# Tiles that begin at a multiple of 256 bytes: filling up the first pool on each side of SBUF

## The chip, the cores and the metric

One NeuronCore of a Trainium2 chip runs the whole kernel. The metric is the device time of one execution in microseconds (us). A changed kernel is compared with the kernel before by the ratio of their times.

## The reference

Three layers run one after the other, all in float32.

```python
# attention with a sigmoid: batch 4, 12 heads, 448 positions, head size 64
scores = scale * q @ k.T - log(448)
attn = 1 / (1 + exp(-scores))
x = (attn @ v) laid out as [1792 tokens, 768]
# max of three products, then an output product (768 x 768 each)
h = max(x @ w1, x @ w2, x @ w3)
x = h @ w_out
# a layer with a leaky slope per column (768 x 2048 and 2048 x 768)
h = x @ w_in
g = max(h, 0) + alpha * min(h, 0)
out = g @ w_out2
```

The weights arrive as float64, which the kernel reads as pairs of 32-bit words and turns into float32 itself.

## The kernel before, in words

All matmuls of the two feed-forward layers are products of float32 numbers that were split into a high and a low part of type fp32r. Each product is three matmuls: high by low, low by high, high by high. A matmul has a **stationary** operand, 128 columns that a weight load (LDWEIGHTS) brings in, and a **moving** operand whose columns are then streamed past it. There is one weight load for each matmul.

The stages are named after their PSUM tiles:

- attention, up to about 146 us: `sc` (scores, L461, moving operand `qh` or `ql`, two matmuls side by side on 64 rows each) and `pav` (L482, plain float32, moving operand `a`);
- `b`, 146 to 399 us (`product`, L641, through `group`, L599 to L604): 1,134 matmuls with 448 moving columns. Names `b_0X`, `b_1X` and so on carry the half g = 0 or g = 1 of the batch as their number. The moving operand is `x_...h` or `x_...l`, the stationary one `f_...h` or `f_...l`;
- `c`, 376 to 467 us (`c_group`, L696): 432 matmuls with 448 moving columns, moving operand `h_...`;
- `d` and `e`, 467 to 933 us, eight rounds: `d` (`d_group`, L833) streams `yh` or `yl`, 512 columns in 948 matmuls and 256 columns in 120; `e` (`e_tile`, L856) streams `g_...`, 512 columns in 864; `e_short` (L884) streams 384 columns of weights in 192.

Weights come in through `wr` (L97 to L117, DMAs on SP's queue); ACT and DVE turn them into `wt` and split them (L177 to L217). `hd` and `hr` (L636, L689) park one intermediate in DRAM and fetch it back.

**Where the tiles lie.** SBUF is filled from two sides, and every pool places its tiles in multiples of 32 bytes of a partition's row. On the left stand the DMA scratch (`SCRATCH`, 4,096 bytes), four constants of 32 bytes each, and then the pool `const` (L63, from byte 4,224): `bias_s` takes 32 bytes, `alpha_sb` and `nalpha` 64 each. So everything behind it begins at 4,384 = 17 x 256 + 32: `wpool` (all weights, raw and split), then `slots_b` and, in its place later, `gpool`. All their tiles are multiples of 256 bytes long, so each begins 32 bytes behind a multiple of 256. On the right the first pool ends at byte 229,344 = 895 x 256 + 224 and is filled downward: `slots_a`, then `apool` and later `slots_c`; `ypool` takes their place for the last layer. These tiles begin 224 bytes behind a multiple of 256, and those of `apool` below the 16-byte tile `gate` (`kh`, `kl` and `zeros`) 192 bytes behind one.

So the moving operand of a matmul begins 32 bytes behind a multiple of 256 in `e`, in `c`, and in `b` for g = 0; 224 bytes behind one in `d`, in the `sc` and `pav` of attention, and in part of `b` for g = 1 (L288: r = 1 lies in `slots_a`, r = 2 mostly in `slots_c`). The stationary operand of `b`, `c` and `d`, and of `e` outside `e_short`, lies in `wpool`, at 32. Slices within a tile begin at multiples of 256 bytes from its start.

The order of the instructions is fixed by the program: a list of products (L737 to L747), and a queue of small operations that are issued between them by credits (`advance`, L135).

Of the kernel before, what the change touches and what calls it, by code (L numbers as in the profile page):

```python
# [9 lines left out]
F32 = mybir.dt.float32  # L10
# [6 lines left out]
P = 128  # L17
# [4 lines left out]
def kernel(  # L22
# [26 lines left out]
    KF2 = DF2 // P  # L49
# [11 lines left out]
    neg_log_s = -math.log(S)  # L61

    const = ctx.enter_context(tc.tile_pool(name="const", bufs=1))  # L63
    wpool = ctx.enter_context(tc.tile_pool(name="wpool", bufs=1))
    pools = {}
    room = {"a": 28, "b": 48, "c": 24, "y": 4}
# [4 lines left out]
    def wslot(nm, dt=F32):  # L71
        return wpool.tile([P, HF], dt, tag="ws", name=nm, bufs=23)

    bias_s = const.tile([P, 1], F32, name="bias_s")
    alpha_sb = const.tile([P, KF2], F32, name="alpha_sb")
    nalpha = const.tile([P, KF2], F32, name="nalpha")

# [242 lines left out]
    def attention(apool, ps_s, ps_v):  # L322
# [187 lines left out]
        nc.vector.memset(bias_s, neg_log_s)  # L510
        zeros = apool.tile([P, 512], BF16, tag="zeros", name="zeros")
        nc.vector.memset(zeros, 0.0)
        gate = apool.tile([P, 4], F32, tag="gate", name="gate")
        ident = apool.tile([P, P], F32, tag="ident", name="ident")
        nc.gpsimd.memset(ident, 0.0)
        nc.gpsimd.affine_select(
# [449 lines left out]
    with tc.manual_schedule():  # L966
        dpool = ctx.enter_context(tc.tile_pool(name="hstore", bufs=1, space=bass.MemoryType.DRAM))
        right = ExitStack()
        pools["a"] = right.enter_context(tc.tile_pool(name="slots_a", bufs=1, side="right"))
        with tc.tile_pool(name="slots_b", bufs=1) as pools["b"]:  # L970
            with (
                tc.tile_pool(name="apool", bufs=1, side="right") as apool,
                tc.tile_pool(name="ps_s", bufs=3, space=bass.MemoryType.PSUM) as ps_s,
                tc.tile_pool(name="ps_v", bufs=2, space=bass.MemoryType.PSUM) as ps_v,
            ):
                attention(apool, ps_s, ps_v)
            ps_m = ctx.enter_context(
                tc.tile_pool(name="ps_m", bufs=8, space=bass.MemoryType.PSUM, reuse_waits="tile")
            )
            pools["c"] = right.enter_context(  # L980
                tc.tile_pool(name="slots_c", bufs=1, side="right", reuse_waits="tile")
            )

            def swap():
                right.close()
                pools["y"] = ctx.enter_context(
                    tc.tile_pool(name="ypool", bufs=1, side="right", reuse_waits="tile")
                )

            z0 = ff1(ps_m, dpool, swap)  # L990
        with tc.tile_pool(name="gpool", bufs=1, reuse_waits="tile") as gpool:
            ff2(gpool, ps_m, z0)
# [39 lines left out]
```

## Time and profile before

| | before |
|---|---|
| median of 3 runs | 942.4 us (940.82 to 943.27) |
| the profiled execution's own time | 942.17 us |
| its span, from the first to the last instruction | 940.4 us |
| PE (matmul) busy | 927.1 us, 99% |
| DVE, ACT, POOL busy | 613.8, 446.8, 71.7 us |
| granted TensorE clock | 0.999 |

A busy PE is one with matmuls in flight. Their ends are modelled and they overlap, so the pace of a stage is read from the starts of its matmuls: time of a stretch divided by the matmuls in it. [...]

### The profile page before, as it was taken

What the parts mean: (1) busy time and instruction counts of PE and PEld (TensorE: products, weight loads), DVE (VectorE), ACT (ScalarE), POOL (GpSimd) and SP (SyncE); (2) the same over time, 40 slices, a digit from 0 to 9 for tenths busy, and PEclk for the clock granted to TensorE, in tenths of its full rate; (3) what the DMA queues carried; (4) which work ended last, traced back from release to release, by engine and by line L of the source; (5) the groups of instructions that cost most, each with busy time, mean ns of one, the idle gap of its engine ahead of it and who ended that gap; (6) DMA issues with size and microseconds to landing.
All of it is one profiled execution on the core that took longest, in us unless ns stands there. A gap on an engine that the chain in (4) does not pass through costs nothing.

```text
span 940.4 us, 12606 instructions
## 1 busy us (share of the span) xinstructions
PE 927.1 (99%) x4712; PEld 758.5 (81%) x4712; DVE 613.8 (65%) x1187; ACT 446.8 (48%) x878; POOL 71.7 (8%) x115
## 2 busy tenths in 40 slices
PE   8999989999999999999999999999999999999997
PEld 5555547999999999899988888888888888888886
DVE  5888885776566568743464466686666866568675
ACT  5878886534433446433366550634506345163410
POOL 4433310001001001100000000000000000000001
PEclk9999999999999999999999999999999999999999
DMA  8999670423114224321221211212112121122027
GB/s 147 141 163 143 114 122 17 118 82 115 49 46 136 68 68 146 112 65 37 68 68 51 67 35 51 67 51 68 34 51 68 51 69 32 51 68 60 25 58 178
DMA packets 148573, 74.24 MB, mean 79 GB/s; under 512 B 94128, under 2 KB 144656, under 8 KB 148512
## 3 DMA queue, kind: packets, MB, share of 16 engines
q1 hardware_dynamic: 140704, 57.60, 27.1%
q0 software_dynamic: 5664, 14.98, 5.7%
q10 hardware_dynamic: 2144, 0.85, 0.4%
q8 instruction: 37, 0.61, 0.3%
q14 instruction: 24, 0.20, 0.1%
HBM read 64.23 MB, written 9.18 MB: 78 GB/s over the span
## 4 chain that ended last, share of the span: by engine, by line
PE 94%; DVE 2%; DMA 1%; ACT 1%; SPq 1%; issue 0%; DVEq 0%; ACTq 0%
PE d L601 25%; PE e L601 21%; PE c L601 9%; PE b_0X L601 7%; PE b_1X L601 7%; PE sc L461 5%; PE pav L482 5%; PE b_0W L601 4%; PE e_short L903 4%; PE b_1W L601 3%; PE b_0V L601 2%; PE b_1V L601 2%; DMA kr<-in_k_dram 1%; ACT a L472 1%; SPq L402 1%
## 5 line engine op out<-in xcount | busy, mean ns | idle before, releaser
L817 DVE SCALAR_TENSOR_TENSOR r<-n,nalpha,r 128x512 f32<-128x512 f32 (+1 forms) x64 | 43.1, 683 | 106.1 <-ACT n L814 106.1
L876 DVE TENSOR_TENSOR acc<-e,acc 128x512 f32<-128x512 f32 x126 | 86.7, 688 | 24.1 <-PE e L601 21.9
L813 ACT ACTIVATE r<-d 128x512 f32<-128x512 f32 (+1 forms) x50 | 29.6, 591 | 152.5 <-PE d L601 152.5
L472 ACT ACTIVATE a<-sc,bias_s 128x896 f32<-128x896 f32 x84 | 82.1, 1015 | 15.1 <-PE sc L461 14.9
L482 PE MATMUL pav<-a,vt 128*64 128x448 f32 (+1 forms) x384 | 70.3, 551 | 0.0
L185 ACT ACTIVATE wt<-wr 128x384 f32<-128x384 f32 x112 | 61.9, 553 | 12.6 <-DMA wr<-in_moe_w_dram 6.3
L200 DVE CUSTOM_DVE_ANT_0 wt<-wr,wt 128x768 uint16<-128x768 uint16 x112 | 62.5, 558 | 3.9
L192 DVE SCALAR_TENSOR_TENSOR wr<-wr 128x384 uint32<-128x384 uint32 x112 | 62.0, 554 | 1.1
L188 ACT ACTIVATE wr<-wr 128x384 uint32<-128x384 uint32 x112 | 61.8, 552 | 0.0
L482 PEld LDWEIGHTS pav<-a,vt 128*64 128x64 f32 (+1 forms) x384 | 21.0, 135 | 38.6 <-issue 35.4
L191 DVE TENSOR_SCALAR wt<-wt 128x384 uint32<-128x384 uint32 x112 | 39.8, 356 | 14.2 <-ACT wt L185 14.2
L931 POOL DMA_DIRECT2D out_dram<-o x6 | 3.9, 660 | 531.3 <-DVE o L851 531.3
L461 PE MATMUL sc<-qh,kh 64*128 64x448 f32 x192 | 38.3, 395 | 4.6 <-DVE qh L435 2.4
L722 DVE TENSOR_TENSOR yl<-c,yh 128x448 fp32r<-128x448 f32 (+5 forms) x36 | 14.1, 421 | 41.5 <-ACT yh L718 29.8
L383 POOL DMA_DIRECT2D vt<-in_v_dram x46 | 35.3, 770 | 65.3 <-PE pav L482 65.3
L461 PEld LDWEIGHTS sc<-qh,kh 64*128 64x128 f32 x192 | 18.1, 184 | 23.2 <-issue 5.6
L718 ACT CAST yh<-c 128x448 fp32r<-128x448 f32 (+5 forms) x36 | 12.1, 375 | 50.1 <-PE c L601 50.1
L461 PE MATMUL sc<-ql,kh 64*128 64x448 f32 x192 | 35.7, 368 | 0.0
L461 PE MATMUL sc<-qh,kl 64*128 64x448 f32 x192 | 35.4, 365 | 0.0
L814 ACT ACTIVATE n<-d 128x512 f32<-128x512 f32 (+1 forms) x50 | 29.2, 583 | 0.0
L670 ACT COPY u<-b_0X 128x448 f32<-128x448 f32 x18 | 9.6, 535 | 38.6 <-PE b_0X L601 38.6
L236 DVE TENSOR_TENSOR u<-b_0W,u 128x448 f32<-128x448 f32 x12 | 7.5, 624 | 30.5 <-ACT u L670 25.7
(1834 smaller groups left out, 2671.5 us busy)
## 6 DMA issues: line engine op xcount, KB each, us to landing
wr<-in_moe_w_out_dram SPq DMA_DIRECT2D x44, 384.0 KB, 3.7
wr<-in_moe_w_dram SPq DMA_DIRECT2D x36, 384.0 KB, 3.8
wr<-in_moe_w_in_dram SPq DMA_DIRECT2D x32, 384.0 KB, 3.6
kr<-in_k_dram SPq DMA_DIRECT2D x92, 56.0 KB, 3.8
qr<-in_q_dram SPq DMA_DIRECT2D x92, 56.0 KB, 3.7
vt<-in_v_dram POOLq DMA_DIRECT2D x46, 96.0 KB, 4.1
hd<-mx POOLq DMA_DIRECT2D x16, 224.0 KB, 2.2
hr<-hd POOLq DMA_DIRECT2D x16, 224.0 KB, 3.9
```

The lines of the kernel that those rows point to most:

```text
L185: nc.scalar.activation(st["T"].bitcast(F32), st["r"][:, :, 1].bitcast(F32), AF.Abs, scale=2.0**-112)
L188: nc.scalar.activation(st["r"][:, :, 0], st["r"][:, :, 0], AF.Copy, scale=2.0**-29)
L191: nc.vector.tensor_scalar(st["T"], st["T"], 3, None, ALU.logical_shift_left)
L192: nc.vector.scalar_tensor_tensor(out=st["r"][:, :, 0], in0=st["r"][:, :, 1], scalar=0x80000000, in1=st["r"][:, :, 0], op0=ALU.bitwise_and, ...
L200: nc.vector.tensor_tensor(out=st["T"], in0=st["r"][:, :, 0], in1=st["T"], op=ALU.add)
L461: nc.tensor.matmul(sc[:, j, :S], kx[r, c0 : c0 + P], qx[r], start=(start and z == 0), stop=(stop and z == 2),)
L472: nc.scalar.activation(a, sc[:, :, :S], AF.Sigmoid, bias=bias_s, scale=scale)
L482: nc.tensor.matmul(pv[i][j * D : (j + 1) * D, :S], vts[i][r, j, c, :], a[r, j, :], start=start, stop=stop,)
L601: nc.tensor.matmul(ps[:, : rh.shape[-1]], lt, rh, start=(start and z == 0), stop=(stop and z == len(mms) - 1), skip_group_check=True,)
L817: nc.vector.scalar_tensor_tensor(out=r_, in0=n_, scalar=nalpha[:, m : m + 1], in1=r_, op0=ALU.mult, op1=ALU.add,)
L876: nc.vector.tensor_tensor(out=acc[m, t], in0=ps, in1=acc[m, t], op=ALU.add)
L903: nc.tensor.matmul(ps, lt, rh, start=(f == 0 and i == 0), stop=(f == SK - 1 and i == 2))
```

## The change

The pool `const` is cut to `bias_s`, which is widened to 128 bytes; `alpha_sb` and `nalpha` move to a new pool `edge` that is the first on the right, 64 + 160 = 224 bytes; the tile `gate` grows from 16 to 256 bytes. With that the left side's pools begin at 4,352 = 17 x 256 and the right side's first large pool ends at 229,120 = 895 x 256. All tiles of `wpool`, `slots_a`, `slots_b`, `slots_c`, `apool`, `ypool` and `gpool` begin at a multiple of 256. No instruction is added, removed or moved, every wait stays, and the sizes that are read and written stay the same.

```diff
     const = ctx.enter_context(tc.tile_pool(name="const", bufs=1))
+    edge = ctx.enter_context(tc.tile_pool(name="edge", bufs=1, side="right"))
     wpool = ctx.enter_context(tc.tile_pool(name="wpool", bufs=1))
...
-    bias_s = const.tile([P, 1], F32, name="bias_s")
-    alpha_sb = const.tile([P, KF2], F32, name="alpha_sb")
-    nalpha = const.tile([P, KF2], F32, name="nalpha")
+    bias_s = const.tile([P, 32], F32, name="bias_s")[:, :1]
+    alpha_sb = edge.tile([P, KF2], F32, name="alpha_sb")
+    nalpha = edge.tile([P, 40], F32, name="nalpha")[:, :KF2]
...
-        gate = apool.tile([P, 4], F32, tag="gate", name="gate")
+        gate = apool.tile([P, 64], F32, tag="gate", name="gate")
```

## Rows read from the trace of the kernel before

**Rows 1.** The page's busy times (share, count) and granted clock in 40 slices.
```profile
PE 927.1 (99%) x4712; PEld 758.5 (81%) x4712; DVE 613.8 (65%) x1187; ACT 446.8 (48%) x878; POOL 71.7 (8%) x115
...
PEclk9999999999999999999999999999999999999999
```

**Rows 2.** What PE's matmuls waited for: us in total, times, longest us.
```profile
PE sc L461 <- DVE qh L435: 2.4, 2, 1.8
PE sc L461 <- ACT f_2h L211: 1.5, 1, 1.5
...
PE e_short L903 <- ACT g L823: 1.1, 1, 1.1
```

**Rows 3.** The chain that ended last, in order of time: start us, us, what.
```profile
172.51 3.64 PE b_1X L601 x18
...
382.21 14.89 PE c L601 x72
399.04 68.16 PE c L601 x335
...
521.14 4.31 PE e_short L903 x24
...
554.89 24.51 PE e L601 x108
...
874.98 25.19 PE d L601 x108
...
924.67 4.25 PE d L601 x36
```

**Rows 4.** The same chain asked for 140 to 380 us: stage b, half 0.
```profile
249.69 1.86 PE b_0X L601 x9
```

**Rows 5.** PE in order of time within e: start us, us, engine, line, operation.
```profile
560.42 0.39 PE L601 MATMUL e<-g_0l,w61h 128*128 128x512 f32 x1
560.65 0.39 PE L601 MATMUL e<-g_0h,w61h 128*128 128x512 f32 x1
560.88 0.39 PE L601 MATMUL e<-g_0h,w63l 128*128 128x512 f32 x1
```

**Rows 6.** The same within d.
```profile
530.42 0.39 PE L601 MATMUL d<-yh,w56l 128*128 128x512 f32 x1
530.66 0.39 PE L601 MATMUL d<-yl,w56h 128*128 128x512 f32 x1
530.89 0.39 PE L601 MATMUL d<-yh,w57l 128*128 128x512 f32 x1
```

**Rows 7.** Weight loads of b and of e_short: ns min/median/max, first and last start.
```profile
L601 PEld LDWEIGHTS b_0X<-x_1h,f_0l x9: 187/188/188, 146.7 to 352.7; 128*128 128x128 f32 x9
...
L903 PEld LDWEIGHTS e_short<-w52h,g x4: 188/188/188, 521.0 to 523.3; 128*128 128x128 f32 x4
```

**Rows 8.** Stretches: us, busy PE, PEld, DVE, ACT, POOL; clock, DMA share, GB/s.
```profile
68.00:100.00 32.00, 32.00 (x234) 17.77 (x234) 26.99 (x52) 26.38 (x36) 11.51 (x17) 1.00 1.06 141
...
120.00:124.00 4.00, 2.69 (x16) 0.77 (x12) 3.79 (x8) 4.00 (x8) 2.92 (x5) 1.00 0.84 179
...
150.00:200.00 50.00, 50.00 (x246) 45.91 (x245) 39.05 (x78) 25.37 (x55) 0.00 (x0) 1.00 0.22 64
500.00:900.00 400.00, 400.00 (x1810) 332.98 (x1809) 254.69 (x475) 171.54 (x361) 0.00 (x0) 1.00 0.18 53
```

**Rows 9.** DVE's subtraction that reads the tile hr, per quarter.
```profile
L215 DVE TENSOR_TENSOR h_0l<-hr,h_0h x4: 615/617/618, 362.5 to 365.1; 128x448 fp32r<-128x448 f32 x4
...
L215 DVE TENSOR_TENSOR h_2l<-hr,h_2h x4: 614/616/618, 388.8 to 391.9; 128x448 fp32r<-128x448 f32 x4
```

**Rows 10.** DMA issues of hr, 353 to 365 us, then 390 to 400: KB, us to landing.
```profile
hr<-hd POOLq DMA_DIRECT2D x8, 224.0 KB, 4.3
...
hr<-hd POOLq DMA_DIRECT2D x4, 224.0 KB, 2.9
```

## The prediction

> **What bounds the kernel now.** I read the page's busy times first: PE is busy for 927.1 of 940.4 us, at the full clock in all 40 slices [rows 1]. So DVE (65%) and ACT (48%) can at most cost PE its remaining 13.3 us. Of those, the view of PE's waits names only a few: 2.4 us on `qh`, 1.5 us on `f_2h`, 1.1 us at the end [rows 2]; the rest is the start before the first scores and the last adds and stores. There is no wait that a change of addresses could remove for more than these few us. Whatever moves the time must move the **pace of the matmuls**.
>
> The pace is read from the chain of waits, as length over count [rows 3, 4]. With 512 moving columns `e` runs at 24.51 / 108 = 226.9 ns and `d` at 25.19 / 108 = 233.2 ns. The same stages in order of time show that this is no average over hiccups: starts stand 0.23 us apart one after the other [rows 5, 6]. With 448 columns `b_0` needs 1.86 / 9 = 206.7 ns, `b_1` 3.64 / 18 = 202.2, early `c` 14.89 / 72 = 206.8, late `c` 68.16 / 335 = 203.5. [...]
>
> [...] Second, `d` and `e` differ by 6.3 ns although shape, type and stationary pool are the same; what differs in the code is that the moving tile begins 224 bytes behind a multiple of 256 in `d` and 32 bytes behind one in `e`. [...]
>
> **The change, part by part.** No instruction, wait or transfer is added or moved. Four terms are left.
>
> 1. *Matmuls of b, c, d and e.* If a matmul no longer touches the extra block, it saves one step of 6.67 ns. There are 1,134 + 432 + 948 + 120 + 864 = 3,498 of them: 23.3 us. [...] I take one step, because one is what the rows show as a difference between two places (`d` against `e`).
>
> 2. *e_short and sc.* `e_short` runs at 179.6 ns with loads of 188 ns, so the load is likely to hold it: I take 0 of its 192 x 6.67 = 1.3 us. `sc` streams 288 pairs, so at most 1.9 us; but from 68 to 100 us the DMA share is 1.06 [rows 8], so a faster PE would meet its loads there: 0.
>
> 3. *Transfers and waits.* `hr` is loaded into the left side (eight issues, 4.3 us to landing) and into the right (four of eight shown, 2.9 us) [rows 10]; the side with the larger offset isn't the slower one, so I take 0. Bound: PE lacks 4.00 - 2.69 = 1.3 us of the stretch from 120 to 124 us, where loads and conversions are late [rows 8], and 13.3 us in all; of these only the waits of [rows 2] in attention, 3.9 us, could hang on a load.
>
> 4. *DVE and ACT.* The same subtraction takes 617 ns on the left tile and 616 on the right [rows 9]: 0. They hide behind PE and still do when PE is 2.5% faster: DVE is busy 39.05 of 50 us in `b` and 254.69 of 400 in `d` and `e` [rows 8].
>
> Sum, against the profiled execution's own 942.17 us: 942.2 - 23.3 = 918.9, taken as **919 us**. That execution is 0.2 us from the median of 942.4, so the same number stands for the median. Own range of this case: 915, with `sc` and `e_short` added (3.2 us), to 930, if only the 1,932 matmuls of `d` and `e` gain (12.9 us).
>
> [...]
>
> **The rivals.**
>
> - *Nothing happens.* [...] For it: late `c` at 203.5 ns and early `c` at 206.8 stream from the same pool with the same offset, and the step between them comes after a stall at 397 us [rows 3], so at least part of the pace is a matter of phase and not of place. Against it: `d` is slower than `e` all along. Time: 942 us. [...]
> - *Only d gains.* What counts is that moving and stationary tile lie at different offsets (224 and 32) in `d` and at the same in `e`. Then `d` takes `e`'s pace, 948 x 6.3 = 6.0 us, and nothing else gains: 936 us. Against it: `b_1`, partly with different offsets, is faster than `b_0`.
> [...]
> - *Slower.* Each stage has two paces, and the change sets the wrong one: `e` takes the pace of `d` (864 x 6.3 = 5.4 us), and `b_1` and late `c` take that of `b_0` (567 x 4.5 + 335 x 3.2 = 3.6 us), since with all tiles at the same offset within 256 the streams of both sides always meet the same part of the memory. That gives 942.2 + 9.0 = 951 us. It decides if `d`, with 948 matmuls, doesn't win its 6.0 us at the same time. For it: `b_0`, where moving and stationary tile share the offset, is the slow one of `b`. Against it: so do they in `e`, which is faster than `d`.
> - *The change doesn't do what it says.* By the sizes in the diff every large pool begins on the boundary; only small tiles (`nalpha`, `bias_s`, at 64 and 128) don't, and no matmul reads them. I give this no chance of its own.
>
> **How the numbers follow.** One step 0.33, two steps 0.12, only `d` 0.15, nothing 0.29, slower 0.11. A measurement of this kernel tells from no change what exceeds about 0.3%, 2.8 us. So faster 0.33 + 0.12 + 0.15 = 0.60, same 0.29, slower 0.11. Forecast 919. The range goes from 895 (two steps) to 944 (nothing, with its scatter of 1.3 us); it leaves out the slower case and the far end below 895. Signs are mixed, so the forecast's own range of 915 to 930 stands beside it.
>
> **What would show it right or wrong.** Right: in the chain `e` at 220 ns and `d` at 220 to 227 per matmul of 512 columns, `b` and `c` at 196 to 200, the stages in the same order and DVE and ACT at the same durations. Two steps: `e` near 214. Only `d`: `d` at 227 and `e` unchanged. Nothing: all paces as in [rows 3, 4]. Slower: `e` at 233. The forecast is wrong if the paces stay and the time still moves; then it was the transfers of attention, and the waits on `qh` and `f_2h` would have changed.

## The result and the profile after

| | before | after |
|---|---|---|
| median | 942.3 us (4 runs) | 932.0 us (929.27, 929.37, 934.59, 935.70) |
| the profiled execution's own time | 942.17 us | 934.59 us |
| its span | 940.4 us | 932.8 us |

The ratio is 0.9895, interval 0.9849 to 0.9941: faster by 1.05%, where 919 us (2.5%) was forecast. The four times of after stand in two pairs 5 to 6 us apart, and the profiled execution belongs to the later pair; this turns out to matter.

The chain that ended last, in order of time (start us, us, what), cuts the span into stages. Of before, the rows that are not shown ahead:

```profile
121.86 5.07 DMA kr<-in_k_dram
...
146.47 2.05 PE b_0X L601 x9
...
467.20 29.43 PE d L601 x132
...
933.39 2.17 DVE accs L914 x4
```

The same view of after (its lines stand 3 higher, L601 is now L604):

```profile
119.17 3.94 DMA kr<-in_k_dram
...
142.63 2.05 PE b_0X L604 x9
...
168.86 3.72 PE b_1X L604 x18
...
380.90 14.89 PE c L604 x72
397.74 68.16 PE c L604 x335
465.91 28.74 PE d L604 x132
...
552.16 24.49 PE e L604 x108
576.64 4.31 PE e_short L906 x24
...
868.52 24.48 PE d L604 x108
...
926.28 2.17 DVE accs L917 x4
```

From the starts of `b`, `d` and the last add:

| stretch | before, us | after, us | gain, us |
|---|---|---|---|
| attention, to the start of b | 146.47 | 142.63 | 3.84 |
| b and c, to the start of d | 320.73 | 323.28 | -2.55 |
| d and e, to the last add | 466.19 | 460.37 | 5.82 |
| last add to the end of the execution | 8.78 | 8.31 | 0.47 |
| sum | 942.17 | 934.59 | 7.58 |

Three things are to be seen [against rows 3]. `d` went from 25.19 to 24.48 us for 108 matmuls, 233.2 to 226.7 ns: it now runs at the pace of `e`. `e` (24.51 to 24.49), `e_short` (4.31), early `c` (14.89) and late `c` (68.16) did not move. `b_1` became slower: 3.64 to 3.72 us for 18, 202.2 to 206.7 ns, which is the pace of `b_0` [rows 4].

Attention, which was to gain nothing, gained half as much again as `b_1` lost. In PE's waits (us in total, times, longest us) the row on `DVE qh` with 2.4 us [rows 2] is gone:

```profile
PE sc L464 <- ACT f_2h L214: 1.3, 1, 1.3
...
PE e_short L906 <- ACT g L826: 1.1, 1, 1.1
```

The stretch in which the loads of attention compete, in the columns of [rows 8] (the last three are clock, DMA share, GB/s; the share adds up the packets' times over the time of 16 engines and can pass 1), moves the same bytes in less of the DMA engines' time, 0.78 instead of 1.06:

```profile
68.00:100.00 32.00, 32.00 (x234) 17.44 (x234) 25.44 (x49) 25.77 (x36) 11.92 (x17) 1.00 0.78 142
```

The page's DMA parts say it for the whole span (a queue's packets, MB and share of the 16 engines' time; then issues, KB each, median us from issue to landing). Of before:

```profile
q1 hardware_dynamic: 140704, 57.60, 27.1%
q0 software_dynamic: 5664, 14.98, 5.7%
...
kr<-in_k_dram SPq DMA_DIRECT2D x92, 56.0 KB, 3.8
...
vt<-in_v_dram POOLq DMA_DIRECT2D x46, 96.0 KB, 4.1
```

Of after:

```profile
q1 hardware_dynamic: 140704, 57.60, 24.5%
q0 software_dynamic: 5664, 14.98, 4.8%
...
kr<-in_k_dram SPq DMA_DIRECT2D x92, 56.0 KB, 2.9
...
vt<-in_v_dram POOLq DMA_DIRECT2D x46, 96.0 KB, 3.2
```

Packets and bytes are the same; K lands in 2.9 instead of 3.8 us, V in 3.2 instead of 4.1. DVE (613.3 us) and ACT (446.4 us) are within 0.5 us of before, and the granted clock is 0.999 in both profiles.

### The profile page after: what moved, and what is told of

Read it like the earlier page. It is cut to its first block, busy times and chain, and to the rows that moved or that the text cites. A ratio compares the mean times of both kernels' runs of the same rounds, so it can differ in the third digit from the quotient of the medians.

```text
span 932.8 us, 12606 instructions
## 1 busy us (share of the span) xinstructions
PE 922.8 (99%) x4712; PEld 758.7 (81%) x4712; DVE 613.3 (66%) x1187; ACT 446.4 (48%) x878; POOL 71.7 (8%) x115
## 4 chain that ended last, share of the span: by engine, by line
PE 96%; ACT 2%; DMA 1%; DVE 1%; issue 0%; SPq 0%; ACTq 0%; DVEq 0%
PE d L604 25%; PE e L604 21%; PE c L604 9%; PE b_0X L604 7%; PE b_1X L604 7%; PE pav L485 6%; PE sc L464 6%; PE b_1W L604 4%; PE b_0W L604 4%; PE e_short L906 4%; PE b_1V L604 2%; PE b_0V L604 2%; ACT a L475 1%; DMA kr<-in_k_dram 0%; DMA kn<-in_k_dram 0%; DVE accs L917 0%
## 5 line engine op out<-in xcount | busy, mean ns | idle before, releaser
L464 PEld LDWEIGHTS sc<-qh,kh 64*128 64x128 f32 x192 | 18.0, 184 | 20.6 <-ACT a L475 6.1
```

The costliest lines, as they stand in the source:

```text
L464: nc.tensor.matmul(sc[:, j, :S], kx[r, c0 : c0 + P], qx[r], start=(start and z == 0), stop=(stop and z == 2),)
```

## The experiments

Four theories were set against each other.

- **P, place** (the prediction's): a moving tile that begins off a boundary costs its own stream a step.
- **D, difference**: what counts is the offset of the moving tile against that of the stationary one, within 256 bytes; equal offsets are fast wherever they lie.
- **T, transfers**: short runs of a DMA into SBUF that cross a multiple of 256 bytes cost more.
- **F, two paces**: the 448-column streams have two paces, 206.7 and 202.7 ns, and which one they take is not fixed by the addresses.

In the labels, "left" and "right" give how far the tiles of each side begin behind a multiple of 256 (before: 32 and 224; after: 0 and 0). In `d` the stationary tile is on the left and the moving one on the right; in `e` both are on the left. Each ratio is to the kernel before, run on the same chip. The edits are shown against the changed kernel, where not said otherwise; each run has one profile.

**One side aligned at a time.** The left alone:

```diff
-    nalpha = edge.tile([P, 40], F32, name="nalpha")[:, :KF2]
+    nalpha = edge.tile([P, 48], F32, name="nalpha")[:, :KF2]
```

> Only the left side is moved to 0 behind a multiple of 256; the right side stays at 224 (apool too). Theory P (place: a matmul's pace depends on where its own moving tile begins): d stays at 233 ns, b_1 at 202. Theory D (difference: what counts is whether moving and stationary tile begin at the same offset): the same here, d 233 and b_1 202. Theory T (transfers: loads into the right side whose 128-byte runs cross a multiple of 256 take longer under load): attention ends near 146.5 us with a DMA share above 1.0 from 68 to 100 us, as before. Rival T0 (the transfers gained from the left side, or by chance): attention ends near 142.6. Time by P, D and T: 942; by T0: 938.

Measured: 939.88 us, ratio 0.9996 (0.9987 to 1.0006): nothing. The right alone:

```diff
-    bias_s = const.tile([P, 32], F32, name="bias_s")[:, :1]
+    bias_s = const.tile([P, 40], F32, name="bias_s")[:, :1]
```

> Only the right side is moved to 0; the left stays at 32. Theory P: d falls to 226.7 ns and b_1 rises to 206.7, as in the changed kernel. Theory D: moving 0 against stationary 32 are unequal, so d stays at 233 and b_1 at 202. Theory T: attention ends near 142.6 us with a DMA share of 0.8. T0: near 146.5. Time by P and T: 932; by D and T: 936.5.

Measured: 938.57 us, ratio 0.9977 (0.9968 to 0.9987). The chain shows `d` unmoved in both, the left alone first, the right alone below:

```profile
873.99 25.20 PE d L604 x108
899.20 24.51 PE e L604 x108
```

```profile
872.78 25.20 PE d L604 x108
```

Aligning either operand of `d` gives `d` nothing, and `e`, with both operands aligned in the first of the two, stays at 24.51: P fell here. The 0.23% of the right alone doesn't come from PE's pace either: in its profile `d` and `e` take 466.26 us (before: 466.19) and `b` and `c` 322.43 us (320.73), while attention ends at 142.54 us (146.47). In the window of 68 to 100 us it has the DMA share of after:

```profile
68.00:100.00 32.00, 32.00 (x236) 17.44 (x234) 25.84 (x50) 25.84 (x36) 11.90 (x18) 1.00 0.80 147
```

**Equal offsets, not aligned.** Both sides at 32:

```diff
-    bias_s = const.tile([P, 32], F32, name="bias_s")[:, :1]
+    bias_s = const.tile([P, 40], F32, name="bias_s")[:, :1]
...
-    nalpha = edge.tile([P, 40], F32, name="nalpha")[:, :KF2]
+    nalpha = edge.tile([P, 32], F32, name="nalpha")[:, :KF2]
```

> Both sides at 32 behind a multiple of 256: equal, but no tile begins on a multiple of 64. Theory D: d 226.7 ns and b_1 206.7. Theory P, if an offset of 32 costs a matmul no more than 0 (as e showed): the same; if the right side's tiles are charged for any offset: d 233. Theory T: every second 128-byte run crosses a multiple of 256, so attention ends near 146.5 us. Time by D and T: 936; by P with a charge for every offset: 942.

Measured: 931.17 us, ratio 0.9898 (0.9883 to 0.9913). Its chain and its window:

```profile
864.40 24.48 PE d L604 x108
888.89 24.48 PE e L604 x108
```

```profile
68.00:100.00 32.00, 32.00 (x234) 17.43 (x234) 25.95 (x50) 25.81 (x36) 11.90 (x18) 1.00 1.01 139
```

`d` has the whole gain with no tile on a boundary, and the transfers have none of theirs (share 1.01). This separates D from T. Two of the figures expected missed: attention ends at 143.38 us and not near 146.5, and `b_1` takes 202.8 ns (line below) and not 206.7; the time is 5 us below the 936 of D and T:

```profile
169.10 3.65 PE b_1X L604 x18
```

**The part of D alone, on the kernel before.** The edit is against the kernel before. In `swap()`, ahead of the pool `ypool`, 192 bytes are put in, which moves the moving operand of `d` from 224 to 32 and no operand of attention, `b` or `c`:

```diff
+                spare = ctx.enter_context(tc.tile_pool(name="spare", bufs=1, side="right"))
+                spare.tile([P, 48], F32, name="spare")
```

> The kernel before with one thing changed: 192 unused bytes ahead of ypool, so that the tiles d streams begin at 32 like its weights, and not at 224. Everything else lies as before. Theory D (difference): d falls from 233.4 to 227 ns, all other paces and the attention stay: 5.8 us less, about 936.5. Theory P (place, with 256-byte boundaries): d stays, 942.

Measured: 934.46 us, ratio 0.9931 (0.9916 to 0.9946), which is 6.5 us; the stretch of `d` and `e` in its profile is 5.80 us shorter than before's. All seven rounds of 132 matmuls of `d` in the chain are at 28.71 or 28.76 us, where those of before are at 29.43; the share from 68 to 100 us stays at 1.06. These two lines give more than half of what the change gives.

Not all else stayed, although its addresses did: attention ends at 143.96 us, and `b` and `c` take 321.82 us, 1.09 more than in before's profile. The groups of `b_0` begin at 1.82 us for 9 and go over to 1.86 from 164 us on, with no stall between, and late `c` is at 69.50 us where before's is at 68.16:

```profile
149.63 1.82 PE b_0X L601 x9
...
180.71 1.86 PE b_0X L601 x9
...
396.28 69.50 PE c L601 x335
```

**Other differences.** The left stays at 0. The right side at 128:

```diff
-    nalpha = edge.tile([P, 40], F32, name="nalpha")[:, :KF2]
+    nalpha = edge.tile([P, 72], F32, name="nalpha")[:, :KF2]
```

> Left at 0, right at 128 behind a multiple of 256. Theory D with the difference counted within 256: d 233 ns and b_1 202. Theory D counted within 64 or 128: d 226.7 and b_1 206.7. Theory P with blocks of 64 or 128 bytes: d 226.7. Theory T: 128-byte runs at 128 and 0 cross no multiple of 256, so attention ends near 142.6 us. Time with d 226.7: 932; with d 233: 936.5.

Measured: 937.01 us, ratio 0.9961 (0.9950 to 0.9973). The right side at 64:

```diff
-    nalpha = edge.tile([P, 40], F32, name="nalpha")[:, :KF2]
+    nalpha = edge.tile([P, 24], F32, name="nalpha")[:, :KF2]
```

> Left at 0, right at 64. Every second 128-byte run crosses a multiple of 256, though all begin at multiples of 64. Theory T (crossing a multiple of 256 is what costs): packets of 128 bytes at 16.8 ns on the mean, attention ends near 145 us. Rival T64 (beginning off a multiple of 64 is what costs): packets 12.7 ns, attention ends near 142.6. Theory D counted within 256 or 128: d at 233 ns; counted within 64: d at 227. Time with T and D: 941.

Measured: 933.59 us, ratio 0.9927 (0.9907 to 0.9946). The right side at 32:

```diff
-    nalpha = edge.tile([P, 40], F32, name="nalpha")[:, :KF2]
+    nalpha = edge.tile([P, 32], F32, name="nalpha")[:, :KF2]
```

> Tiles on the left at 0, on the right at 32 behind a multiple of 256: the offset of the right tile minus that of the left is 32. Theory D (the pace of d goes by that difference, 227.5 ns at 0, 229.4 at 64, 232.3 at 128, 233.4 at 192): d near 228.5 ns for 512 columns. If what counts is how far apart the two are in either direction, 32 is the same as 224, and d is at 233.5 ns. Theory T (128-byte runs that cross a multiple of 256 are slow): DMA share at 68 to 100 us near 1.0, attention ends at 143 to 145 us. e at 226.9 ns whatever d does. Time 931 to 935 us by D, 938 to 940 us by the other.

Measured: 937.78 us, ratio 0.9972 (0.9960 to 0.9983). The last round of `d`, right at 128:

```profile
870.21 25.10 PE d L604 x108
```

Right at 64:

```profile
866.28 24.73 PE d L604 x108
```

Right at 32:

```profile
870.49 25.19 PE d L604 x108
```

The expectation of 228.5 ns for 32 missed: it is 233.2. At 64 both values expected, 233 and 227, missed: it is 229.0, and the time is 7 us below the 941 of T and D. The pace does not grow with the difference. Equal offsets give 24.48 us, and all five differences that were tried cost more: 25.19 (32), 24.73 (64), 25.10 (128), 25.19 (192, before) and 25.20 (224). What order lies in these five is open.

At 64 and 32 the window of 68 to 100 us is at 1.00 and 1.05, at 128 it is at 0.79, although 64 and 128 are both multiples of 64. Runs of 128 bytes cross a multiple of 256 from 32, 64 and 224, and do not from 0 and 128: so T divides the runs rightly, in the share and in the packets' times (16.4 ns in the mean at 64, where T64 had 12.7).

Two things limit this. Attention ended at 142.19 us at 64, the time of T64 and not the 145 of T, so the share doesn't fix the end of attention in a single profile. And a run of 128 bytes that begins at a multiple of 128 never crosses a multiple of 256, so these runs can't tell T from a rule that a start off a multiple of 128 is what costs. The packet records have 896 packets of 256 bytes, the first loads of V: 18.0 ns in the mean in each of the six runs with the right side at 0 or 128, 20.6 to 22.9 in the others. From 128 each of them crosses a multiple of 256 and pays nothing for it, which speaks for 128.

**Both sides at 128.**

```diff
-    bias_s = const.tile([P, 32], F32, name="bias_s")[:, :1]
+    bias_s = const.tile([P, 64], F32, name="bias_s")[:, :1]
...
-    nalpha = edge.tile([P, 40], F32, name="nalpha")[:, :KF2]
+    nalpha = edge.tile([P, 72], F32, name="nalpha")[:, :KF2]
```

> Both sides at 128 behind a multiple of 256: equal, and no 128-byte run crosses a multiple of 256. Theories D, T and F: as the changed kernel, d 227 ns, 128-byte packets 12.7 ns, attention ends near 142.6 us, b at one pace of 202.7 or 206.7; time near 929 or near 934.5. If beginning at a multiple of 256 had a worth of its own: slower than that by 2 us or more.

Measured: 929.22 us, ratio 0.9876 (0.9860 to 0.9893), profiled execution 929.14 us. `d` is at 24.48 us for 108, the share at 0.79. So 128 serves as well as 0, for both parts.

**The changed kernel again, twice.** No edit.

> The changed kernel once more, unchanged. Theory F (with equal offsets, b keeps one of two paces, 202.7 or 206.7 ns, from its first matmul to its last, and which one is drawn at its start): the times fall into two groups 5 us apart, near 929.3 and near 934.5, and the profile shows b at 202.7 if its own time is in the lower group, at 206.7 if in the upper. Rival (scatter comes from the transfers of attention): b at 206.7 whatever the time, and the start of b differs by 5 us instead.

Measured: 928.65, 929.08, 930.07 and 930.44 us, ratio 0.9880 (0.9865 to 0.9895), profiled execution 929.08 us.

> The changed kernel once more, for the two paces of b and c. Theory F (a pace of 206.7 or 202.7 ns is set where PE starts b and kept until it stalls): each execution lands near 929.4 us or near 935 us and none halfway, and the profiled one shows all of b at one of the two paces, with 206.7 ns if its time is near 935 us. Rival (the pace drifts within b): times spread evenly between 929 and 935 us and b shows both paces. d at 227.5 ns and the DMA share at 68 to 100 us near 0.78 in either case.

Measured: 929.33, 929.56, 929.82 and 934.34 us, ratio 0.9894 (0.9869 to 0.9919), profiled execution 929.56 us. Of twelve executions of this kernel nine lie between 928.65 and 930.44 us, three between 934.34 and 935.70, and none between; of the three late ones only after's first has a profile. The chain of the first of the two, beside that of after above:

```profile
141.56 2.02 PE b_0X L604 x9
...
167.29 3.65 PE b_1X L604 x18
...
392.27 68.16 PE c L604 x335
460.43 28.74 PE d L604 x132
...
863.05 24.48 PE d L604 x108
...
920.80 2.17 DVE accs L917 x4
```

The same instructions at the same addresses give 3.65 / 18 = 202.8 ns in `b_1` here and 206.7 in after, and the other groups of `b` in this chain are at 1.82 or 1.83 us for 9 where those of after are at 1.86: F. The 1,134 matmuls of `b` at 4 ns are 4.5 us of the 5.4 us between the means of the two groups of times, 929.5 and 934.9 us. The first group of nine in `b` already shows which pace it is (2.02 or 2.05 us), and it holds until PE stalls: late `c`, which begins behind a stall, is at 68.16 us in both. What sets the pace at the start of `b` was not tried.

F is about streams with equal offsets. The five profiles with both sides equal have `b_0` and `b_1` at one pace, within 0.1 ns of each other: four at 202.6 or 202.7 ns, after at 206.6. In the seven profiles with unequal offsets, where part of `b_1` is unequal, the two differ by 1.2 to 4.4 ns, and not always the same way: by the starts of their matmuls `b_0` and `b_1` take 206.4 and 202.7 ns before, 206.1 and 201.7 with the right at 64, 202.3 and 204.4 with it at 32. Of that last one:

```profile
180.15 1.82 PE b_0X L604 x9
181.97 1.85 PE b_1X L604 x9
```

So the level is not fixed by the addresses, but a difference between `b_0` and `b_1` goes with them. Late `c` has two paces as well: 68.16 us in ten profiles, 69.50 and 69.49 in `d_alone` and the right alone, behind the same stall.

**All runs side by side.** The pace of `d` is that of its 512-column matmuls in the last round of 108; the share is that of 68 to 100 us; `b` starts where attention ends.

| left, right | ratio | d, ns | DMA share | b starts, us |
|---|---|---|---|---|
| 32, 224 (before) | 1 | 233.2 | 1.06 | 146.47 |
| 0, 224 | 0.9996 | 233.3 | 1.12 | 145.08 |
| 0, 32 | 0.9972 | 233.2 | 1.05 | 143.29 |
| 0, 64 | 0.9927 | 229.0 | 1.00 | 142.19 |
| 32, 224, `d` at 32 | 0.9931 | 226.7 | 1.06 | 143.96 |
| 32, 32 | 0.9898 | 226.7 | 1.01 | 143.38 |
| 32, 0 | 0.9977 | 233.3 | 0.80 | 142.54 |
| 0, 128 | 0.9961 | 232.4 | 0.79 | 142.46 |
| 128, 128 | 0.9876 | 226.7 | 0.79 | 141.80 |
| 0, 0 (after; again; third) | 0.9895; 0.9880; 0.9894 | 226.7 | 0.78 | 142.63; 141.56; 142.09 |

The six profiles with a share of 1.00 and more start `b` at 144.1 us in the mean, the six with 0.78 to 0.80 at 142.2: by these means the transfers are worth some 1.9 us, and before's own profile was a late one of its kind. The two sets overlap (142.19 in the first, 142.63 in the second), so this is an estimate. No version beat the changed kernel by more than the noise.

## Why the prediction was wrong

**Term 1 failed**: "If a matmul no longer touches the extra block, it saves one step of 6.67 ns", for all 3,498 fp32r matmuls of `b`, `c`, `d` and `e`, 23.3 us. The median of 932 us lies in the range of 895 to 944, but that range also holds "nothing happens" and says little; it lies outside the forecast's own 915 to 930, and that the faster executions, near 929.5, fall inside is luck, since other causes brought them there. No run shows the step of 6.67 ns, nor the extra block; what the runs show in its place is 6.5 ns a matmul in 864 matmuls of `d`, and at most 0.2 ns in `e`. Measured, by stage:

- `d`: 233.2 to 226.7 ns, 5.82 us for the stretch of `d` and `e`. The step of 6.3 to 6.5 ns between `d` and `e` was read rightly and explained wrongly. It is the price of unequal offsets of the two operands, not of a start off a boundary: equal offsets of 0, 32 and 128 all stand at 226.7 ns. Nor did all 948 gain: 864 did, 5.6 us; the other 84, which alternate with the matmuls of 256 columns, stand at 234 to 235 ns in both profiles.
- `e`: 0, 226.9 to 226.8 ns. Its operands had equal offsets all along, so by D there was nothing to win; at 0, 32 and 128 its groups of 108 take 24.48 to 24.53 us in all twelve profiles.
- `b` and `c`: -2.55 us in after's profile, +1.86 us in the chain of `after_again` (460.43 - 141.56 = 318.87 against 320.73). Which it is goes by the pace taken at the start of `b`.

**The rivals.** "Only d gains" named the right condition for `d`, with 6.0 us against 5.8 measured. The objection to it, that `b_1` with partly different offsets is faster than `b_0`, read a true row: unequal offsets cost `d` 6.5 ns and did not cost `b_1` that (202.7 ns before, by the starts of its matmuls), and D doesn't say why. It failed as an objection because `b_0` stood at the slower of its two paces (206.4 ns), and because the experiments on `d` decide for `d` alone. "Slower" was half right: after's `b_1` did take the pace of `b_0`, for 567 x 4.5 = 2.55 us, just the price given, though by the pace that this execution happened to take; but `e` kept its pace, and in the two other profiles of the changed kernel `b_1` doesn't take it (202.8 ns); the reason given for this rival was not shown. "Nothing happens" had a remark that held, that the step of `c` behind a stall is no matter of place: it goes from 206.8 to 203.5 ns in before's profile, at offset 32, and in after's, at 0.

**Term 2**: `e_short` 0, as taken. `sc` gained a little: groups of 30 went from 3.28 to 3.24 us, 1.3 ns for each of 576 matmuls, 0.8 us. Before, `kh` was at 192 and `qh` at 224; the groups are at 3.24 wherever the two are equal (0, 32, 64, 128 and 224 on the right) and at 3.28 in the run with only `d` changed. That fits D in a second stage; no other unequal pair was run there.

**Term 3 failed too**: transfers at 0. Its bound of 3.9 us held, but nothing was taken from it. The reason given, that `hr` lands no later on the side with the larger offset [rows 10], compared long rows on two sides that were both off the boundary. The transfers that changed are K, Q and V of attention, in short runs, and they were not priced. The trace's packet records have 82,432 packets of 128 bytes for K and Q, in the mean 16.7 ns before and 12.7 after (16.4 to 17.3 in all runs with a share of 1.00 and more, 12.6 to 12.9 in the others), and 1,104 of 2,048 bytes for V, 144 and 91 ns. That this reaches the end is best seen in the right side alone, which gains 0.23% with no gain in `d`, `b` or `c`. The chain agrees: the last load of `kr` ends at 126.93 us before and at 123.11 after, 3.82 us earlier, as much as the whole stage; but 2.7 of these us were there when it began, and before's profile was a late one. The packets of 128 bytes are slow from 64, at 16.4 ns, and fast from 0 and 128, at 12.6 to 12.9; those of 256 bytes take 18.0 ns from 128 as from 0. So the runs show that the start in SBUF counts, and 128 fits them all.

**Term 4**, DVE and ACT, was right at 0.

**The sum as it should have been**: 5.8 for `d`, some 1.9 for transfers and `sc` together, 0.5 at the end, and +1.9 or -2.6 for `b` and `c` by the pace: 10.1 or 5.6 us of 942. The gain of before to `after_again` by their own profiles, 942.17 - 929.08 = 13.09 us, is larger by the 3 us that before's attention was late and `after_again`'s early within their kinds.

## What to carry to other kernels

Where two operands of a long series of fp32r matmuls come from pools on different sides of SBUF, compare their offsets within 256 bytes: making them equal gave 5.8 us here, and a multiple of 256 was not needed for it. Where a load writes short runs, ask whether they begin at a multiple of 128 bytes in SBUF: the 128-byte runs that did took a quarter less time, 12.7 against 16.7 ns in the mean. Before the paces of two stages are compared, look whether one stage has the same pace in several executions; here one stage took 202.7 or 206.7 ns with the same addresses.

## What was not expected of the hardware

- The pace of `d` is not monotonic in the difference of the offsets: 226.7 ns at 0, 229.0 at 64, 232.4 at 128, 233.2 at 32 and 192, 233.3 at 224. Differences of 96 and 160 were not tried, nor equal offsets other than 0, 32 and 128.
- One stream of 1,134 matmuls, with the same addresses, equal offsets and no wait in it, runs at 202.7 or at 206.7 ns throughout, as it was set within its first group of nine. This gives the changed kernel most of the distance between its two times, some 929.5 and 934.9 us.
- Unequal offsets cost `d` up to 6.5 ns a matmul, but `b_1` is the faster half of `b` with them in six of seven profiles.
- Effects of the two sides do not add up: the left alone 0.04%, the right alone 0.23%, both 1.05 to 1.2%, since equality is a property of the pair.
